# Attention, MoE and SoLU-MoE in one program: another order for the scores of the last 64 queries, two score maxima, one exponential and a weight rounding within the attention's repeating period

## The chip, the cores and the metric

The program runs on one core of a Trainium2 chip. The metric is the device time of the whole program in microseconds (us). Before the change its median is 817.85 us over 3 runs (817.72 to 817.94).

## What is computed

Three layers follow one another; only the first is touched.

```
scores = (1/sqrt(D)) * q @ k^T, causal, minus the row maximum     # B=4, H=8, S=576, D=64
a      = exp(scores); a /= a.sum(-1) + 1e-9
local  = a @ v
mem    = (phi(q) @ M_prev) / (phi(q) . z_prev + 1e-6)             # phi(x) = max(x, exp(min(x,0)) - 1) + 1
attn   = g * mem + (1 - g) * local,   g = sigmoid(beta) per head
x      = attn as (B*S, H*D)                                       # 2304 tokens x 512
x      = (h - tanh(h)) @ w_out,  h = x @ w_in                     # d_ff 2048
out    = LayerNorm(h * softmax(h)) * g_ln @ w_out2                # d_ff 1024
```

## The kernel before

**Tiling.** The 32 heads are taken in 16 pairs, two heads of 64 dimensions side by side on 128 partitions; a pair has the number i from 0 to 15. The 576 queries of a head fall into four blocks c = 0 to 3 of 128 queries and one last block of 64. The causal scores of block c are 128(c+1) wide; those of the last block are 576 wide, and both heads' 64 rows share one tile S_L. A tile of weights P carries both the index c and the head j of its pair as i = 2c + j, and i = 8 (LAST) is the tile of the last 64 queries of both heads.

**Software pipeline.** The order of all work on the attention is written out by hand, as a PROLOGUE and then a PERIOD, a list of 80 steps that `run` repeats for p = 4 to 19. A step reads `name:at:engine:part` and acts on the pair p + at. So one pass over PERIOD computes the scores of pair p-1, normalises and transposes the weights of pairs p-2 and p-3, multiplies those of p-3 with v, and stores the result of p-4. Each engine works through its own instructions in the order of that list; semaphores make it wait where a tile isn't ready.

**The steps that matter here,** in the names of the list, with the lines of the profile:

- `s_r:c` (L274, TensorE): scores of block c of both heads, each product in two passes, on halves of 64 rows of the array ("64*128" in the rows). `s_r:1` does blocks 1 and 0. `s_r:3` is 512 wide, `s_r:2` 384, `s_r:1` 256 and 128.
- `s_l` (L288, TensorE): scores of the last 64 queries, on quarters of the array ("64*64").
- `s_max:i` (L298, VectorE): adds the mask, scales, writes the scores to SBUF and takes each row's extreme. It is the reader that frees the scores' PSUM tile.
- `s_exp:i` (L320, ScalarE): the exponential with the row's maximum, and the row's sum.
- `s_eps` (L331, GpSimd) and `s_inv` (L335, VectorE): the sums plus 1e-9, and their reciprocal; part 0 is for i = 6 to 8, part 1 for i = 0 to 5.
- `s_norm:i` (L344, GpSimd): the weights times reciprocal and gate.
- `a_t:g` (L384, TensorE): transposes weights into PSUM in groups g = 0 to 5; `a_ev:g` (L391, ScalarE) copies such a group to SBUF and so frees its PSUM tile. Group 3 needs `s_norm` 3, 5 and 7, group 1 also `s_norm` 1, group 0 `s_norm` 0, 2, 4 and 6.
- `a_pv` (L408, TensorE): the transposed weights times v, into the tile X; `a_mem` (L366), `m_mm` (L225): the memory part. `x_ev` (L432): X to SBUF.
- `q_t`, `k_t` (L192, VectorE), `f_neg` (L207, GpSimd), `f_exp` (L210, ScalarE), `f_max` (L214, VectorE): q and k transposed, and phi(q) as min, exp, max.
- `w:0` to `w:8`: one conversion of a piece of MoE weights from 64-bit words into a rounded part and a remainder, in every fourth pair (i = 2, 6, 10, 14). `w:0` is on ScalarE, `w:1` to `w:5` on VectorE, `w:6` (L793) on GpSimd, `w:7` (L800, the rounding copy) on ScalarE, `w:8` (L802, the remainder) on GpSimd. `w:6` to `w:8` fall into the periods p = 6, 10, 14 and 18.
- `room`: places where the split of x for the MoE layer puts single steps (L582 on ScalarE, L584 on GpSimd).

**PSUM.** All eight banks are given out: tag S has two tiles of two banks, tag T two tiles of one bank, X one of two banks. A tile that is asked for takes the place that was given out longest ago, and the first instruction that writes it waits for the last reader of what was there. In one period, tag S is asked for by `a_t:5`, `m_mm`, `s_r:3`, `s_l`, `s_r:2`, and tag T by `a_t:0`, `a_t:2`, `a_t:4`, twice by `s_r:1` (a tile for each head), `a_t:3`, `a_t:1`. So the two tiles of `s_r:1` take the places of `a_t:2` and `a_t:4`:

```
        if c == 1:
            t = [
                self.ps.tile([P, 512], F32, tag="T", name=f"S{p}_{c}{j}", bufs=2)
                for j in range(2)
            ]
        else:
            S = self.ps.tile([P, 1024], F32, tag="S", name=f"S{p}_{c}", bufs=2)
```

After the last period the MoE layers take over; TensorE runs products for their first blocks between the last attention steps.

Of the kernel before, what the change touches and what calls it, by code (L numbers as in the profile page):

```python
# [21 lines left out]
class Attention:  # L22
# [1183 lines left out]
```

## Time and profile before

| | |
|---|---|
| median of 3 runs | 817.85 us (817.72 to 817.94) |
| the profiled execution | 813.16 us |
| its span, first to last instruction | 811.3 us |
| attention, up to its last product with v | about 210 us of the span |
| one period in the middle of it | 11.11 us |

The profile is of one execution, and its times hold for that one. "Busy" of TensorE (PE) counts matmuls whose ends are modelled; PEld are its weight loads. A row of the timeline merges neighbouring instructions of one line (x4 is four instructions), and the bracket behind it is the idle time of the engine before it, with what ended it. The chain of waits follows the work back from the last instruction, at each step to what released it. The granted clock was 0.998 of full speed.

### The profile page before, as it was taken

Reading aid. Unit: us, or ns where it says so; the run is one execution under the profiler, and the core shown is the slowest. Engines: PE = TensorE matmul, PEld = TensorE weight load, DVE = VectorE, ACT = ScalarE, POOL = GpSimd, SP = SyncE. Lnnn points to the kernel's source line nnn. Section 1 sums busy time; section 2 is a strip of 40 time slices with the busy share of each in tenths; the row PEclk is TensorE's granted clock in tenths of the full one; section 3 lists DMA queues with packets and bytes.
Section 4 is the critical chain, followed back from the end, with each engine's and each line's share of the span. In section 5 each row is a group of like instructions: output and inputs, shape, how many; then the busy total and the mean of one; then the engine's idle time right before and its main releaser. Section 6 shows DMA issues by size and latency. Waiting matters only on the chain.

```text
span 811.3 us, 13124 instructions
## 1 busy us (share of the span) xinstructions
PE 787.5 (97%) x4816; PEld 691.6 (85%) x4816; DVE 582.1 (72%) x1101; ACT 349.2 (43%) x712; POOL 375.5 (46%) x394
## 2 busy tenths in 40 slices
PE   3999999999999999999999999999999899999998
PEld 1666766666899999999999999999998688888887
DVE  5888888974377777777777777756877676767663
ACT  3788988886333333232333323232322323323322
POOL 5778898978523333233333324321542443344430
PEclk9999999999999999999999999999999999999999
DMA  8477769781012122121211212110100433333331
GB/s 176 122 171 173 155 129 162 130 168 49 23 52 78 53 57 75 53 78 53 73 58 55 76 53 78 53 53 27 53 27 27 141 106 123 111 130 112 110 116 40
DMA packets 75888, 72.57 MB, mean 89 GB/s; under 512 B 50480, under 2 KB 58416, under 8 KB 75824
## 3 DMA queue, kind: packets, MB, share of 16 engines
q1 hardware_dynamic: 75728, 71.45, 33.4%
q8 instruction: 38, 0.62, 0.3%
q10 hardware_dynamic: 96, 0.29, 0.1%
q14 instruction: 26, 0.21, 0.1%
HBM read 54.41 MB, written 12.58 MB: 83 GB/s over the span
## 4 chain that ended last, share of the span: by engine, by line
PE 87%; DVE 4%; DMA 3%; POOL 2%; ACT 2%; issue 2%; SPq 1%; DVEq 0%; ACTq 0%; POOLq 0%
PE Y L644 24%; PE H L615 24%; PE H L839 11%; PE S L274 4%; PE T L384 4%; PE X L408 4%; PE S_L L288 2%; PE R L225 2%; DVE sc L298 1%; POOL xT L584 1%; DMA v<-in_v_dram 1%; PE X L366 1%; PE O16S L939 1%; PE O1X L939 1%; PE O14X L939 1%
## 5 line engine op out<-in xcount | busy, mean ns | idle before, releaser
L644 PE MATMUL Y<-G,wo 128*128 128x384 f32 x1152 | 207.9, 335 | 0.2 <-DVE yT L656 0.2
L644 PEld LDWEIGHTS Y<-G,wo 128*128 128x128 f32 x1152 | 200.7, 188 | 0.5 <-ACT xh L582 0.4
L615 PE MATMUL H<-xh,wi 128*128 128x384 f32 x768 | 157.5, 337 | 0.0
L793 POOL TENSOR_TENSOR cvw<-cvw,cva 128x512 f32<-128x512 f32 x48 | 62.1, 1293 | 179.0 <-DVE cva L791 136.5
L615 PEld LDWEIGHTS H<-xh,wi 128*128 128x128 f32 x768 | 135.4, 188 | 1.4 <-issue 1.4
L628 ACT ACTIVATE t<-H 128x768 f32<-128x768 f32 x48 | 39.1, 814 | 211.4 <-PE H L615 211.4
L344 POOL TENSOR_SCALAR P<-P,sm,og 128x128 f32<-128x128 f32 (+3 forms) x128 | 82.0, 652 | 21.9 <-DVE sm L335 19.0
L839 PE MATMUL H<-w2i,Ys 128*128 128x512 f32 x384 | 89.9, 390 | 0.0
L615 PE MATMUL H<-xT,wi 128*128 128x384 f32 x384 | 89.7, 337 | 0.0
L839 PEld LDWEIGHTS H<-w2i,Ys 128*128 128x128 f32 x384 | 72.1, 188 | 15.0
L629 DVE TENSOR_TENSOR t<-H,t 128x768 f32<-128x768 f32 x48 | 45.9, 957 | 52.6 <-ACT t L628 52.6
L658 DVE TENSOR_TENSOR yT<-Y,yT 128x384 f32<-128x384 f32 (+1 forms) x126 | 78.9, 681 | 0.0
L631 DVE TENSOR_TENSOR G<-t,G 128x768 fp32r<-128x768 f32 x48 | 46.5, 968 | 43.3 <-ACT G L630 43.3
L320 ACT ACTIVATE P<-sc,mx 128x128 f32<-128x128 f32 (+3 forms) x128 | 70.7, 554 | 8.5 <-DVE mx L298 8.4
L298 DVE CUSTOM_DVE_ANT_0 sc<-S,mask 128x128 f32<-128x128 f32 (+3 forms) x128 | 55.5, 485 | 21.4 <-PE S L274 21.4
L615 PEld LDWEIGHTS H<-xT,wi 128*128 128x128 f32 x384 | 68.4, 188 | 0.2 <-issue 0.2
L630 ACT CAST G<-t 128x768 fp32r<-128x768 f32 x48 | 40.1, 835 | 51.2 <-DVE t L629 51.2
L391 ACT COPY pt<-T 128x512 f32<-128x512 f32 (+1 forms) x95 | 53.9, 603 | 15.9 <-PE T L384 15.5
L274 PE MATMUL S<-kT,qT 64*128 64x256 f32 (+3 forms) x256 | 46.5, 488 | 14.1 <-DVE kT L192 14.1
L871 POOL TENSOR_TENSOR s<-s,nhalf 128x1 f32<-128x1 f32 x18 | 9.9, 552 | 101.2 <-DVE s L870 92.2
L856 ACT ACTIVATE e<-H,s 128x1024 f32<-128x1024 f32 x18 | 20.1, 1116 | 80.5 <-DVE s L850 77.7
L408 PE MATMUL X<-pt,v 128*64 128x64 f32 (+4 forms) x576 | 48.2, 319 | 0.4 <-ACT pt L391 0.4
(270 smaller groups left out, 1254.6 us busy)
## 6 DMA issues: line engine op xcount, KB each, us to landing
raw<-in_moe_w_in_dram SPq DMA_DIRECT2D x24, 512.0 KB, 3.7
q<-in_q_dram SPq DMA_DIRECT2D x64, 140.0 KB, 3.0
raw<-in_moe_w_out_dram SPq DMA_DIRECT2D x16, 512.0 KB, 3.3
D<-rest SPq DMA_DIRECT2D x15, 512.0 KB, 2.6
rest<-D SPq DMA_DIRECT2D x60, 128.0 KB, 2.9
out_dram<-ob SPq DMA_DIRECT2D x17, 256.0 KB, 2.9
k<-in_k_dram SPq DMA_DIRECT2D x30, 140.0 KB, 3.6
v<-in_v_dram SPq DMA_DIRECT2D x32, 128.0 KB, 3.8
```

The source lines that it names most:

```text
L274: nc.tensor.matmul(s, Q[rows, P * r : P * r + P], K[rows, 0:w], start=True, stop=True, skip_group_check=True,)
L298: self.nc.vector.tensor_tensor_reduce(out=sc, in0=s, in1=mask, scale=-0.125, scalar=3.0e38, op0=ALU.add, op1=ALU.min, accum_out=self.mx[p] ...
L320: self.nc.scalar.activation(t, self.sc.pop((p, i)), AF.Exp, bias=self.mx[p][:, i : i + 1], scale=-1.0, accum_out=self.sm[p][:, i : i + 1],)
L344: self.nc.gpsimd.tensor_scalar(d, d, self.sm[p][:, i : i + 1], og, ALU.mult, ALU.mult)
L391: self.copy(pt, T)
L408: self.nc.tensor.matmul(self.X[j * D : (j + 1) * D, q0 : q0 + w], v[:, kb, j, :], self.pt[p, gs[j]][:, at[j] : at[j] + w], start=False, st ...
L615: nc.tensor.matmul(H[a:z, f], wi[:, wl, c, f * P + a : f * P + z], self.x[n][xl][:, c], start=(count[f] == 0), stop=(count[f] == 3 * KD - ...
L631: nc.vector.tensor_tensor(G[:, 1], t, G[:, 0].bitcast(F32), ALU.subtract)
L644: nc.tensor.matmul(Y[d][:, 0:NB], wo[:, wl, f, d * P : (d + 1) * P], G[:, gl, f], start=(i == 0), stop=(i == 3 * KF - 1),)
L658: nc.vector.tensor_tensor(y, src, y, ALU.add)
L793: self.eng.tensor_tensor(w, w, a, ALU.add)
L839: nc.tensor.matmul(H[:, nh * 512 : (nh + 1) * 512], Y[:, yl, c, :], w2i[:, wl, c, nh * 512 : (nh + 1) * 512], start=(k == 0), stop=(k == 3 ...
```

## The change

Only the text of PERIOD changes; the set of its 80 steps is the same. Five things move:

- `s_l` goes from ahead of `s_r:1` to behind `s_r:2`, and `s_r:2` goes up to stand right behind `s_r:1`. TensorE's order is `s_r:3`, `s_r:1`, `s_r:2`, `s_l` instead of `s_r:3`, `s_l`, `s_r:1`, `s_r:2`. Tag S is asked for by `s_r:2` ahead of `s_l`.
- On VectorE, `s_max:3` and `s_max:1` go ahead of `s_max:8`, and `s_inv` part 1 of the pair before goes from ahead of `s_max:8` to behind it.
- On ScalarE, `s_exp:3` goes ahead of `s_exp:8`.
- `w:7` goes from ahead of `a_ev:2` to behind `a_ev:4` on ScalarE.
- `w:8` goes from ahead of `s_eps` part 1 to behind `s_norm:3` on GpSimd.

```
-        a_ev:-3:a:1 a_t:-3:-:0 w:-4:-:6 x_ev:-4:v f_neg:-1:p a_ev:-3:a:5 s_exp:-2:-:4
-        w_ld:-2:- a_ev:-3:a:0 k_t:-1:- a_mem:-3:- s_norm:-2:-:7 w:-4:-:7 a_t:-3:-:2
-        a_ev:-3:a:2 m_eps:-2:- s_norm:-2:-:8 a_t:-3:-:4 s_r:-1:-:3 f_exp:-1:- m_inv:-2:- m_mul:-2:-
-        a_ev:-3:a:4 w:-4:-:8 s_l:-1:- s_r:-1:-:1 w:-3:-:3 room:0:-:0
-        s_eps:-2:-:1 s_norm:-2:-:6 load_q:0:s load_k:0:s s_max:-1:-:6
-        s_max:-1:-:7 m_gate:-1:- w:-2:-:0 s_exp:-1:-:6 s_exp:-1:-:7 f_max:-1:-
-        s_inv:-2:-:1 s_max:-1:-:8 s_r:-1:-:2 s_max:-1:-:3 a_pv:-3:-:0 a_pv:-3:-:3
-        a_pv:-3:-:2 s_max:-1:-:1 load_v:-2:s x_mv:-4:- s_norm:-2:-:3 w:-3:-:4
-        s_norm:-2:-:5 s_exp:-1:-:8 s_max:-1:-:2 s_max:-1:-:0 a_pv:-3:-:1 s_max:-1:-:5
-        s_norm:-2:-:1 s_max:-1:-:4 w:-2:-:1 a_t:-2:-:3 s_eps:-1:-:0 s_exp:-1:-:3
+        a_t:-3:-:0 w:-4:-:6 x_ev:-4:v f_neg:-1:p a_ev:-3:a:5 s_exp:-2:-:4 w_ld:-2:-
+        a_ev:-3:a:0 k_t:-1:- a_mem:-3:- s_norm:-2:-:7 a_t:-3:-:2 a_ev:-3:a:2 m_eps:-2:-
+        s_norm:-2:-:8 a_t:-3:-:4 s_r:-1:-:3 f_exp:-1:- m_inv:-2:- m_mul:-2:- a_ev:-3:a:4
+        w:-4:-:7 s_r:-1:-:1 s_r:-1:-:2 w:-3:-:3 room:0:-:0 s_eps:-2:-:1 s_norm:-2:-:6
+        load_q:0:s load_k:0:s s_max:-1:-:6 s_max:-1:-:7 s_l:-1:- m_gate:-1:- w:-2:-:0
+        s_exp:-1:-:6 s_exp:-1:-:7 f_max:-1:- s_max:-1:-:3 s_max:-1:-:1 s_exp:-1:-:3
+        s_max:-1:-:8 s_inv:-2:-:1 a_pv:-3:-:0 a_pv:-3:-:3 a_pv:-3:-:2 load_v:-2:s x_mv:-4:-
+        s_norm:-2:-:3 w:-4:-:8 w:-3:-:4 s_norm:-2:-:5 s_exp:-1:-:8 s_max:-1:-:2 s_max:-1:-:0
+        a_pv:-3:-:1 s_max:-1:-:5 s_norm:-2:-:1 s_max:-1:-:4 w:-2:-:1 a_t:-2:-:3 s_eps:-1:-:0
```

## Rows read from the trace of the kernel before

**Rows 1.** The page, part 1: busy time, share of span, instructions.

```profile
PE 787.5 (97%) x4816; PEld 691.6 (85%) x4816; DVE 582.1 (72%) x1101; ACT 349.2 (43%) x712; POOL 375.5 (46%) x394
```

**Rows 2.** Chain of waits, period p = 4: start us, us, what.

```profile
43.93 1.12 PE S_L L288 x8
...
55.04 1.12 PE S_L L288 x8
```

**Rows 3.** Timeline of TensorE, p = 5: start, us, instructions, idle before.

```profile
49.37 1.09 PE L384 MATMUL T<-ident,P 128*128 128x128 f32 x8
...
53.91 1.13 PE L274 MATMUL S<-kT,qT 64*128 64x512 f32 x4
54.97 1.19 PE L288 MATMUL S_L<-kT,qT 64*64 64x512 f32 x8
56.09 1.57 PE L274 MATMUL S<-kT,qT 64*128 64x256 f32 x12
57.59 2.96 PE L408 MATMUL X<-pt,v 128*64 128x512 f32 x36
```

**Rows 4.** Timeline of ScalarE, p = 5: `a_ev:2`, `f_exp`, `a_ev:4`.

```profile
53.58 0.59 ACT L391 COPY pt<-T 128x512 f32<-128x512 f32 x1 [0.34 <-PE T L384]
54.06 0.69 ACT L210 ACTIVATE e<-e 128x576 f32<-128x576 f32 x1
54.65 0.58 ACT L391 COPY pt<-T 128x512 f32<-128x512 f32 x1
```

**Rows 5.** Chain of waits, p = 11: TensorE resumes behind a copy.

```profile
120.08 0.48 ACT pt L391
...
120.61 0.66 PE T L384 x4
```

**Rows 6.** Timeline of VectorE, p = 5: `s_max:7`, `s_inv:1`, `s_max:8`.

```profile
55.70 0.69 DVE L298 CUSTOM_DVE_ANT_0 sc<-S,mask 128x512 f32<-128x512 f32 x1
...
56.99 0.18 DVE L335 RECIPROCAL sm<-sm 128x6 f32<-128x6 f32 x1
57.09 0.71 DVE L298 CUSTOM_DVE_ANT_0 sc<-S_L,maskL 128x576 f32<-128x576 f32 x1
```

**Rows 7.** Timeline of GpSimd, p = 5 and 6: `s_norm` 3, 5, 1; `f_neg`; `w:8`.

```profile
57.27 1.80 POOL L344 TENSOR_SCALAR P<-P,sm,og 128x256 f32<-128x256 f32 x3 [0.82 <-DVE sm L335]
...
62.84 1.65 POOL L207 TENSOR_SCALAR e<-qT 128x576 f32<-128x576 f32 x1
...
66.01 1.28 POOL L802 TENSOR_TENSOR wi<-cvw,wi 128x512 fp32r<-128x512 f32 x1
```

**Rows 8.** Timeline of GpSimd, p = 9 and 10: the same `s_norm` and `f_neg`.

```profile
102.11 1.80 POOL L344 TENSOR_SCALAR P<-P,sm,og 128x256 f32<-128x256 f32 x3 [0.82 <-DVE sm L335]
...
108.65 1.64 POOL L207 TENSOR_SCALAR e<-qT 128x576 f32<-128x576 f32 x1
```

**Rows 9.** Timeline of ScalarE: `a_ev:4` of p = 9, `f_exp` of p = 10.

```profile
99.09 0.58 ACT L391 COPY pt<-T 128x512 f32<-128x512 f32 x1
...
110.32 0.68 ACT L210 ACTIVATE e<-e 128x576 f32<-128x576 f32 x1 [0.52 <-POOL e L207]
```

**Rows 10.** Who waited for whom: us in total, times, longest us.

```profile
ACT e L210 <- POOL e L207: 9.1, 3, 8.0
```

**Rows 11.** Timeline of TensorE, end of p = 10 to p = 11.

```profile
116.03 1.09 PE L384 MATMUL T<-ident,P 128*128 128x128 f32 x8
...
120.61 0.66 PE L384 MATMUL T<-ident,P 128*128 128x128 f32 x4 [0.40 <-ACT pt L391]
121.19 1.13 PE L274 MATMUL S<-kT,qT 64*128 64x512 f32 x4
```

**Rows 12.** Timeline of ScalarE, p = 18: `w:7`, then `a_ev:2` and `a_ev:4`.

```profile
206.56 0.62 ACT L800 CAST wo<-cvw 128x512 fp32r<-128x512 f32 x1 [1.04 <-POOL cvw L793]
207.09 1.07 ACT L391 COPY pt<-T 128x512 f32<-128x512 f32 x2
```

**Rows 13.** Timeline of TensorE, p = 18: the products behind those copies.

```profile
208.21 1.52 PE L408 MATMUL X<-pt,v 128*64 128x256 f32 x12 [0.35 <-ACT pt L391]
```

More of the change, by code (lines that the diff above doesn't have):

```diff
@@ L473 @@
         q_t:-1:- s_norm:-3:-:4 w:-3:-:2 s_exp:-2:-:0 s_exp:-2:-:5 s_norm:-3:-:0 a_t:-3:-:5
-        s_norm:-3:-:2 m_mm:-2:- room:0:-:2 a_ev:-3:a:3 load_m:-1:- s_inv:-2:-:0
-        a_ev:-3:a:1 a_t:-3:-:0 w:-4:-:6 x_ev:-4:v f_neg:-1:p a_ev:-3:a:5 s_exp:-2:-:4
-        w_ld:-2:- a_ev:-3:a:0 k_t:-1:- a_mem:-3:- s_norm:-2:-:7 w:-4:-:7 a_t:-3:-:2
-        a_ev:-3:a:2 m_eps:-2:- s_norm:-2:-:8 a_t:-3:-:4 s_r:-1:-:3 f_exp:-1:- m_inv:-2:- m_mul:-2:-
-        a_ev:-3:a:4 w:-4:-:8 s_l:-1:- s_r:-1:-:1 w:-3:-:3 room:0:-:0
-        s_eps:-2:-:1 s_norm:-2:-:6 load_q:0:s load_k:0:s s_max:-1:-:6
-        s_max:-1:-:7 m_gate:-1:- w:-2:-:0 s_exp:-1:-:6 s_exp:-1:-:7 f_max:-1:-
-        s_inv:-2:-:1 s_max:-1:-:8 s_r:-1:-:2 s_max:-1:-:3 a_pv:-3:-:0 a_pv:-3:-:3
-        a_pv:-3:-:2 s_max:-1:-:1 load_v:-2:s x_mv:-4:- s_norm:-2:-:3 w:-3:-:4
-        s_norm:-2:-:5 s_exp:-1:-:8 s_max:-1:-:2 s_max:-1:-:0 a_pv:-3:-:1 s_max:-1:-:5
-        s_norm:-2:-:1 s_max:-1:-:4 w:-2:-:1 a_t:-2:-:3 s_eps:-1:-:0 s_exp:-1:-:3
+        s_norm:-3:-:2 m_mm:-2:- room:0:-:2 a_ev:-3:a:3 load_m:-1:- s_inv:-2:-:0 a_ev:-3:a:1
+        a_t:-3:-:0 w:-4:-:6 x_ev:-4:v f_neg:-1:p a_ev:-3:a:5 s_exp:-2:-:4 w_ld:-2:-
[7 more added lines that the diff above has]
+        a_pv:-3:-:1 s_max:-1:-:5 s_norm:-2:-:1 s_max:-1:-:4 w:-2:-:1 a_t:-2:-:3 s_eps:-1:-:0
         a_t:-2:-:1 s_exp:-1:-:2 w:-3:-:5 s_exp:-1:-:1
```

## The prediction

> **What bounds the kernel now.** First the page's busy times [rows 1]: TensorE is busy for 97% of the span, no other engine for more than 72%. That is an average over three layers, so the next view is the chain of waits inside the attention. It runs through TensorE alone for whole periods, and the same step comes back after 55.04 - 43.93 = 11.11 us [rows 2]. TensorE's timeline then shows its instructions of one period end to end without a bracket of idle time [rows 3]. In such a period nothing that another engine saves is worth anything; the period grows by whatever TensorE waits, and shrinks only by what TensorE no longer does. The third view is therefore the waits that stand close behind TensorE: the copies of ScalarE that free PSUM [rows 4], the maxima on VectorE [rows 6] and the GpSimd queue [rows 7, 8]. There are 13 periods, p = 4 to 16, in which scores are computed by PERIOD's order.
>
> **Part 1: the order of the scores on TensorE.** Three things come of it.
>
> *A wait is added.* The two tiles of `s_r:1` take the places of `a_t:2` and `a_t:4`, so its product for the second head can't start before `a_ev:4` has read its place. Before, `s_l` stood between; now `s_r:1` follows `s_r:3` directly, and that ends where `s_l` starts today, at 54.97 [rows 3]. `a_ev:4` ends at 54.65 + 0.58 = 55.23 [rows 4]. It can't be earlier: `a_ev:2` starts when its transposes end (its bracket names them), `f_exp` and `a_ev:4` follow end to end. A resumption of TensorE behind such a copy took 120.61 - (120.08 + 0.48) = 0.05 us [rows 5]. So `s_r:1` restarts at 55.28. Then come `s_r:1` and `s_r:2` with 57.59 - 56.09 = 1.50 and `s_l` with 56.09 - 54.97 = 1.12 [rows 3], and `a_pv` starts at 57.90 instead of 57.59: **+0.31 per period, 13 x 0.31 = +4.0**. Behind the waiting instruction stand `s_r:2`, which is ready, `s_l` and `a_pv`; all of TensorE waits with it.
>
> *A switch falls away, if the wait doesn't eat it.* `s_r:3` streams 2 x 512 columns in 53.91 to 54.97 = 1.06 us, `s_r:1` and `s_r:2` together 2 x (256 + 128 + 384) = 1536 in 1.50 [rows 3]. So 512 columns cost 0.44, and each group has 0.18 that isn't streaming: the turn from another division of the array and the first weight load. With `s_r:1` right behind `s_r:3`, both on halves, that 0.18 could go. But a load that waits for `a_ev:4` isn't hidden, so I keep the full 1.50. The bounds: 0.31 if nothing is hidden, 0.31 - 0.18 = 0.13 if all is. I take 0.31, since the wait sits on the first pair of products. The Trainium skill says under "TensorEngine Tiling (Array Packing)", Key Properties, that changing the tiling mode, not just the tile, drains TensorE. The row's 0.18 agrees with that; by this rule alone one drain fewer would be worth 13 x 0.18 = 2.3 us, and it speaks for the change.
>
> *Later readers.* `s_l` now takes the place of `s_r:3` in tag S and waits for `s_max:7`, which ends at 55.70 + 0.69 = 56.39 [rows 6]; `s_l` comes at 55.28 + 1.50 = 56.78, so this is hidden. `a_t:5` now waits for `s_max:4` in place of `s_max:8`. `s_max:8` ends some 3.45 us behind the restart (below), `a_t:5` comes at 5.5 + 1.0 (8 transposes, 1.09 with their tail [rows 3]); 3.0 us hold `s_inv` and four maxima, none as wide as the 0.71 of `s_max:8`. Hidden too.
>
> **Part 2: the maxima and the reciprocal.** `s_max:8` now waits for `s_l`, which ends at 56.78 + 1.19 = 57.97 instead of 54.97 + 1.19 = 56.16. `s_max:3`, `s_max:1` and `s_exp:3` fill the gap on VectorE and ScalarE and cost nothing. What stands behind `s_max:8` is `s_inv:1`, and GpSimd waits for it ahead of `s_norm` 3, 5 and 1: the bracket of 0.82 [rows 7]. The new time: 57.97 + 0.05 + 0.71 for `s_max:8`, then 57.27 - 56.99 = 0.28 from `s_inv` to `s_norm:3` [rows 6, 7], is 59.0 instead of 57.27. So GpSimd's queue starts **1.7 later in the period**, 3.7 behind the restart. In a normal period this is hidden by GpSimd's idle time. In periods with `w:6` it isn't, since `w:6` stands ahead of `f_neg`, `f_exp` waits for `f_neg`, and `a_ev:4` stands behind `f_exp`:
>
> - p = 6: `f_neg` ends at 62.84 + 1.65 + 1.7 = 66.19 [rows 7]; `f_exp` would start at 54.06 + 11.11 + 0.31 = 65.48 [rows 4]. **+0.7**.
> - p = 10: `a_ev:4` of p = 9 ends at 99.67, so the restart is at 99.72 and `s_norm:3` at 103.42 instead of 102.11: 1.3 later. `f_neg` ends at 108.65 + 1.64 + 1.3 = 111.59 [rows 8, 9]; `f_exp` would start at 99.09 - 0.59 + 11.11 + 0.31 = 109.92. **+1.7**. Already today `f_exp` waits 0.52 there [rows 9], at no cost, because `s_l` covers it.
> - p = 14: the wait for `f_neg` occurs three times, 8.0 of 9.1 us in one of them [rows 10], so the other two are alike. **+1.7**.
>
> **Part 3: the rounding behind the copies.** `w:7` behind `a_ev:4` takes 0.62 us of ScalarE [rows 12] from ahead of `a_ev:2`; in p = 11 and 15 TensorE now loses 121.19 - 116.03 = 5.16 against 53.91 - 49.37 = 4.54, so 0.62 [rows 11, 3], because the maxima and copies run late behind a conversion. I count it all as given back: **-1.2**. In p = 18 the products wait 0.35 for copies that stand behind `w:7` [rows 12, 13]: **-0.35**.
>
> `w:8` now stands between `s_norm:3` and `s_norm:5`, and `a_t:3` at the end of the period needs `s_norm:5`. Counted from the restart: 3.7 + 0.6 (a third of 1.80) + 1.28 + 0.6 = 6.2 [rows 7]; `a_t:3` wants to start at 1.50 + 1.12 + 2.89 = 5.5 (49.37 + 11.11 - 57.59 is the 2.89) [rows 3]. **+0.7 in each of p = 6, 10 and 14: +2.1**. Whether `f_neg` of the next period is then late as well, these rows leave open: 0 to 0.7 each.
>
> No DMA step changes its place on SP's queue, and none is moved past.
>
> **The sum.** 4.0 + (0.7 + 1.7 + 1.7) + 2.1 - 1.2 - 0.35 = +8.65, so +8.6 us. The profiled execution takes 813.16 us with a span of 811.3, so it would become 821.8 with a span of 819.9. The median of the runs is 4.7 above the profiled one; with the same distance it is 817.85 + 8.6 = **826.4**.
>
> **The rivals.**
>
> - *The wait alone.* If GpSimd's queue catches up (its `s_norm` of 1.80 hold stretches in which they share with VectorE, and these would fall elsewhere), parts 2 and 3 add nothing: 4.0 - 1.2 - 0.35 = +2.4, **820.2**. For it: normal periods have idle time on GpSimd [rows 7]; against it: p = 10 is late already today [rows 9].
> - *No wait: the maxima become the bound.* If `a_ev:4` is in time, `s_r:1` and `s_r:2` end at 54.97 + 1.50 - 0.18 = 56.29, `s_l` waits for `s_max:7` until 56.44 and ends at 57.56: -0.03 per period, -0.4. With the stalls given back, -0.4 - 1.2 - 0.35 = -2.0, **815.9**. It decides at an end of `a_ev:4` ahead of 54.97, and it is 0.26 later in the row; only a `f_exp` that goes elsewhere would change that. By the drain rule above with all of its 2.3, the time would be 817.85 - 3.9 = 814.0.
> - *The hidden load.* With 0.13 in place of 0.31 and no late GpSimd: 1.7 - 1.2 - 0.35 = +0.1, **818.0**.
>
> The wait rests on program order: a TensorE instruction that waits isn't passed. In p = 11 TensorE stands idle for 0.40 ahead of `a_t:4` [rows 11], and nothing behind it goes ahead. The Trainium skill states it so under "TensorE: Matmul & The Clock Gate", Part 2, step-by-step: matmuls stay in program order, and only weight loads are pulled ahead. Were it otherwise, `s_r:2` would fill the wait and the +0.31 would shrink towards nothing.
>
> **How the numbers follow.** The forecast has 0.58, the wait alone 0.25, no wait 0.10, the hidden load 0.07. A measurement of this kernel can tell 0.2%, 1.6 us, from no change. So slower has 0.83, same 0.07, faster 0.10. The range reaches down to the wait alone, 820.0, and up by the open lateness of `f_neg`, 3 x 0.7 = 2.1, with a little for the rest: 829.0.
>
> **What would show it.** In the timeline of the changed kernel, the first rows of L274 behind the 512-wide ones should carry a bracket that names ACT pt L391, of 0.2 to 0.4 in most periods; the period in the chain should be 11.4 instead of 11.11; in p = 6, 10 and 14 `f_exp` should wait for `f_neg`, and `a_t:3` for GpSimd's weights. The prediction is wrong if the period stays at 11.11 or below, if `a_ev:4` no longer ends behind `s_r:3`, or if those three periods cost no more than the others.

## The result and the profile after

| | before | after |
|---|---|---|
| median | 816.23 us (6 runs, 813.60 to 817.94) | **824.58 us** (6 runs, 822.86 to 825.67) |
| ratio after to before | | **1.0111**, 95% interval 1.0086 to 1.0137 |
| profiled execution | 813.16 us | 822.87 us |
| its span | 811.3 us | 821.0 us |
| second group of Y products starts (attention done) | 214.93 us | 224.65 us |
| from there to the end | 596.4 us | 596.4 us |

(Three of before's six runs are those of the table ahead of the prediction; the ratio is taken from runs that stand beside each other, and stands for 9.1 us where the two medians differ by 8.35.) The changed kernel is slower by about 1%, and all of it lies in the attention. The page of after, part 1, busy time by engine, shows next to nothing of it:

```profile
PE 793.7 (97%) x4816; PEld 697.3 (85%) x4816; DVE 579.5 (71%) x1101; ACT 351.3 (43%) x712; POOL 376.3 (46%) x394
```

The share of 97% is that of [rows 1], and PE's busy time even grew, by 6.2 us: the page doesn't tell a loss of this kind. The chain of waits of after, in p = 4 and 5 (start us, us, what), says more:

```profile
44.03 2.86 PE S L274 x14
46.89 1.12 PE S_L L288 x8
...
55.44 2.86 PE S L274 x14
```

The step that came back after 11.11 us in [rows 2] comes back after 55.44 - 44.03 = 11.41. All scores of the row blocks take 2.86 where `s_r:3` and the group of `s_r:1` and `s_r:2` took 1.06 + 1.50 = 2.56 [rows 2, 3]: 0.30 more.

TensorE's timeline of after (start, us, instructions, idle before) at the scores of p = 6 and of p = 10, and behind those:

```profile
66.78 1.55 PE L274 MATMUL S<-kT,qT 64*128 64x512 f32 x6
68.67 1.56 PE L274 MATMUL S<-kT,qT 64*128 64x256 f32 x10 [0.33 <-ACT pt L391]
...
113.78 1.55 PE L274 MATMUL S<-kT,qT 64*128 64x512 f32 x6
116.63 1.56 PE L274 MATMUL S<-kT,qT 64*128 64x256 f32 x10 [1.30 <-ACT pt L391]
118.12 1.19 PE L288 MATMUL S_L<-kT,qT 64*64 64x512 f32 x8
119.24 2.96 PE L408 MATMUL X<-pt,v 128*64 128x512 f32 x36
122.13 0.33 PE L384 MATMUL T<-ident,P 128*128 128x128 f32 x1
122.83 1.08 PE L384 MATMUL T<-ident,P 128*128 128x128 f32 x7 [0.38 <-POOL P L344]
```

Four products of `s_r:3` and the two of `s_r:1`'s first head run (x6); the second head's wait for the copy `a_ev:4`, and the ten that are left still take 118.12 - 116.63 = 1.49. In p = 10 there is a second wait, of `a_t:3` for GpSimd's weights. ScalarE's timeline of after shows `a_ev:2`, `f_exp` and `a_ev:4` of those two periods:

```profile
66.45 0.58 ACT L391 COPY pt<-T 128x512 f32<-128x512 f32 x1 [0.34 <-PE T L384]
67.46 0.68 ACT L210 ACTIVATE e<-e 128x576 f32<-128x576 f32 x1 [0.42 <-POOL e L207]
68.05 0.57 ACT L391 COPY pt<-T 128x512 f32<-128x512 f32 x1
...
113.44 0.58 ACT L391 COPY pt<-T 128x512 f32<-128x512 f32 x1 [0.34 <-PE T L384]
115.42 0.68 ACT L210 ACTIVATE e<-e 128x576 f32<-128x576 f32 x1 [1.39 <-POOL e L207]
116.01 0.57 ACT L391 COPY pt<-T 128x512 f32<-128x512 f32 x1
```

`f_exp` waits 0.42 and 1.39 for `f_neg` and holds up `a_ev:4`, which ends at 68.62 and 116.58; TensorE goes on 0.05 later each time, as in [rows 5]. On GpSimd, `s_norm:3` of p = 5 starts late, behind the moved `s_inv:1`, and `f_neg` of p = 6 and 10 ends at 67.43 and 115.38:

```profile
60.44 1.69 POOL L344 TENSOR_SCALAR P<-P,sm,og 128x256 f32<-128x256 f32 x3 [1.01 <-DVE sm L335]
...
65.77 1.66 POOL L207 TENSOR_SCALAR e<-qT 128x576 f32<-128x576 f32 x1
...
113.74 1.64 POOL L207 TENSOR_SCALAR e<-qT 128x576 f32<-128x576 f32 x1
```

Who waited for whom in after, against [rows 10] (us in total, times, longest us):

```profile
ACT e L210 <- POOL e L207: 11.7, 6, 8.0
...
PEld S L274 <- ACT pt L391: 10.3, 26, 1.7
```

The second row is new: two weight loads in each of 13 periods.

**A finer measure than the median.** Within one execution a period without a special wait repeats to 0.01 or 0.02 us, while runs of one kernel spread over some 5 us. So the distance between the starts of successive 512-wide scores (the L274 rows that begin with 64x512, as at 66.78 and 113.78 above) is what the experiments are read by. In us, from one period to the next:

| kernel | normal | 6 to 7 | 9 to 10 | 10 to 11 | 11 to 12 | 14 to 15 |
|---|---|---|---|---|---|---|
| before | 11.11 | 11.11 | 11.11 | 11.73 | 11.11 | 11.74 |
| after | 11.41 | 12.62 | 11.55 | 13.59 | 11.75 | 13.58 |
| e1 | 11.41 | 11.49 | 11.41 | 12.41 | 11.41 | 12.41 |
| e2 | 11.41 | 11.41 | 11.41 | 12.39 | 11.41 | 12.44 |
| e3 | 11.41 | 11.94 | 11.55 | 12.90 | 11.41 | 12.90 |
| e4 | 11.11 | 11.35 | 11.11 | 11.99 | 11.11 | 12.00 |
| e5 | 11.11 | 11.11 | 11.11 | 11.15 | 11.11 | 11.14 |
| e6 | 11.09 | 11.78 | 11.12 | 12.22 | 11.09 | 12.22 |
| e7 | 11.09 | 11.09 | 11.09 | 11.40 | 11.09 | 11.39 |
| e8 | 11.09 | 12.01 | 11.09 | 12.96 | 11.12 | 12.96 |
| e9 | 11.37 | 11.45 | 11.51 | 12.41 | 11.38 | 12.40 |
| e10 | 11.11 | 11.11 | 11.11 | 11.17 | 11.11 | 11.16 |
| e11 | 10.91 | 11.11 | 11.40 | 11.10 | 10.91 | 12.06 |

Conversions fall into p = 6, 10 and 14. Of the distances that the table leaves out, 13 to 14 is like 9 to 10 and 15 to 16 like 11 to 12, and one other stands out by over 0.1: 5 to 6, with 11.27 in e7, 11.54 in e9 and 11.27 in e11.

### The profile page after: what moved, and what is told of

It is laid out like the page before. It is cut to its first block, busy times and chain, and to the rows that moved or that the text cites. A ratio compares the mean times of both kernels' runs of the same rounds, so it can differ in the third digit from the quotient of the medians.

```text
span 821.0 us, 13114 instructions
## 1 busy us (share of the span) xinstructions
PE 793.7 (97%) x4816; PEld 697.3 (85%) x4816; DVE 579.5 (71%) x1101; ACT 351.3 (43%) x712; POOL 376.3 (46%) x394
## 4 chain that ended last, share of the span: by engine, by line
PE 85%; POOL 7%; DVE 3%; issue 3%; ACT 1%; DMA 1%; SPq 0%; DVEq 0%; POOLq 0%; ACTq 0%
PE Y L643 24%; PE H L614 24%; PE H L838 11%; PE S L274 4%; PE T L384 4%; PE X L408 3%; POOL P L344 3%; PE S_L L288 2%; PE R L225 1%; POOL xT L583 1%; POOL e L207 1%; PE X L366 1%; PE O16S L938 1%; PE O1X L938 1%; PE O14X L938 1%
## 5 line engine op out<-in xcount | busy, mean ns | idle before, releaser
L274 PE MATMUL S<-kT,qT 64*128 64x128 f32 (+3 forms) x256 | 51.3, 493 | 17.6 <-DVE kT L192 14.4
L274 PEld LDWEIGHTS S<-kT,qT 64*128 64x128 f32 x256 | 27.0, 204 | 33.3 <-DVE kT L192 13.2
```

Source lines behind the costliest of these rows:

```text
L274: nc.tensor.matmul(s, Q[rows, P * r : P * r + P], K[rows, 0:w], start=True, stop=True, skip_group_check=True,)
```

## The experiments

All of them compute the whole reference; only the order of steps in PERIOD differs (in e11 in PROLOGUE too).

**e1, the order alone.** Before's PERIOD with the new order of scores, maxima and exponential; `s_inv:1`, `w:7` and `w:8` keep their places of before.

```diff
-a_ev:-3:a:4 w:-4:-:8 s_l:-1:- s_r:-1:-:1
+a_ev:-3:a:4 w:-4:-:8 s_r:-1:-:1 s_r:-1:-:2
...
+s_max:-1:-:7 s_l:-1:-
...
-f_max:-1:- s_inv:-2:-:1 s_max:-1:-:8 s_r:-1:-:2 s_max:-1:-:3
+f_max:-1:- s_inv:-2:-:1 s_max:-1:-:3 s_max:-1:-:1 s_exp:-1:-:3 s_max:-1:-:8
...
```

> From the kernel before, only the scores' order and the maxima and the exponential that follow it are changed (s_r:3, s_r:1, s_r:2, s_l; s_max:3, s_max:1, s_exp:3 ahead of s_max:8); s_inv:1, w:7 and w:8 stay where they were before. Theory: the wait of s_r:1 for a_ev:4 alone costs 13 x 0.30 = 3.9 us, and in p = 6, 10 and 14, where a_ev:4 is later behind w:7, another 0.1 + 0.7 + 0.7; so +3.9 to +5.4 against before, and the period is 11.41 in the trace. Rival (GpSimd's late queue is what costs, the order itself is free or a gain): 0 to -2.4, period 11.11 or below.

Measured: 1.0064 (1.0041 to 1.0086), 819.22 against 813.65 us. The normal period has the full +0.30, so the order isn't free. In p = 10 and 14 another 1.00 comes without any step of part 2 or 3. TensorE's timeline of e1 at p = 10, and `a_t:2` and `a_t:4` of p = 11:

```profile
112.56 1.55 PE L274 MATMUL S<-kT,qT 64*128 64x512 f32 x6
114.93 1.56 PE L274 MATMUL S<-kT,qT 64*128 64x256 f32 x10 [0.81 <-ACT pt L391]
116.42 1.19 PE L288 MATMUL S_L<-kT,qT 64*64 64x512 f32 x8
...
124.00 1.04 PE L384 MATMUL T<-ident,P 128*128 128x128 f32 x8
```

In before `f_exp` waits 0.52 there too [rows 9], but `s_l` stood between `s_r:3` and the place that `a_ev:4` frees. Taking it away makes an old, covered lateness visible: two thirds of the 1.48 that p = 10 of after loses by late copies on top of the 0.30 of every period. The scores up to `s_l` take 116.42 - 112.56 = 3.86 here instead of 2.86, which is all of the 1.00. So the stall of before ahead of `a_t:4` in p = 11, 0.62 long with a bracket of 0.40 [rows 11], is gone in e1: the row at 124.00 holds the eight transposes of `a_t:2` and `a_t:4` without a bracket. `w:7` and `w:8` stand there as in before, so the new order of scores is enough to remove the stall.

**e2, the reciprocal back up.** After, with `s_inv:1` right behind `f_max`.

```diff
-f_max:-1:- s_max:-1:-:3 s_max:-1:-:1 s_exp:-1:-:3 s_max:-1:-:8 s_inv:-2:-:1
+f_max:-1:- s_inv:-2:-:1 s_max:-1:-:3 s_max:-1:-:1 s_exp:-1:-:3 s_max:-1:-:8
```

> The changed kernel with s_inv:1 back ahead of the maxima (right behind f_max). Theory: GpSimd's queue starts 1.7 us earlier, f_exp waits for f_neg no longer in p = 6 and by only 0.4 in p = 10 and 14, and w:8 is done in time for s_norm:5, so a_t:3 waits no longer; left are 13 x 0.30 + 0.8 - 1.2 - 0.35 = +3.1 against before. Rival (the conversion's remainder w:8 itself is what is too long for the queue, wherever the reciprocal stands): f_exp and a_t:3 go on waiting, +6 to +8.5.

Measured: p = 6 falls from 12.62 to 11.41, p = 10 from 13.59 to 12.39, p = 14 from 13.58 to 12.44. The span is 815.4, 4.1 above before. By the runs it is 1.0081 (1.0056 to 1.0105), with 820.08, 820.98 and 820.19 us beside the profiled 817.23; the section on the clock has the likely reason why single executions differ by that much. So the place of `s_inv:1` makes GpSimd late, and this costs 1.2 us in each conversion. The 1.0 that is left in p = 10 and 14 was expected at 0.4; it is the uncovered lateness of e1. From e1, e2 differs only in the places of `w:7` and `w:8`, and their distances from p = 6, 10 and 14 agree within 0.08: in the new order these two moves are worth next to nothing as long as `s_inv:1` is early. TensorE of e2 in p = 11 shows that `a_t:3` no longer waits, although `w:8` has after's place:

```profile
116.14 2.96 PE L408 MATMUL X<-pt,v 128*64 128x512 f32 x36
119.03 1.09 PE L384 MATMUL T<-ident,P 128*128 128x128 f32 x8
```

**e3, the remainder right behind the rounding.** After, with `w:8` behind `w:7` instead of behind `s_norm:3`.

```diff
-a_ev:-3:a:4 w:-4:-:7 s_r:-1:-:1
+a_ev:-3:a:4 w:-4:-:7 w:-4:-:8 s_r:-1:-:1
...
-s_norm:-2:-:3 w:-4:-:8 w:-3:-:4
+s_norm:-2:-:3 w:-3:-:4
```

> The changed kernel with w:8 taken from between s_norm:3 and s_norm:5 and put right behind w:7, where GpSimd's queue waits for s_inv:1 anyway. Theory: a_t:3 no longer waits in p = 6, 10 and 14 (0.69 each in the changed kernel's trace) and f_neg of p = 11 and 15 is no longer late (0.34 each): 2.7 less than the changed kernel, the periods of p = 6, 10, 14 at 11.9, 12.9, 12.9 instead of 12.62, 13.59, 13.58; the other periods stay at 11.41. Rival (the wait of a_t:3 comes from the late s_inv:1 alone): 0.0, the same periods.

Measured: 1.0087 (1.0055 to 1.0119); 11.94, 12.90 and 12.90. So 12.62 - 11.94 = 0.68 and twice 0.69 are `w:8`'s place, and so are the 0.34 of p = 11 and 15. Against e2 the rest of `s_inv:1`'s cost is 11.94 - 11.41 = 0.53 and 12.90 - 12.39 = 0.51. The wait of `a_t:3` takes both moves: it is gone in e2, where the queue is early, and in e3, where `w:8` is out of it.

**e4, the rounding alone,** and **e5, the remainder alone,** each from before.

```diff
 e4
-s_norm:-2:-:7 w:-4:-:7 a_t:-3:-:2
+s_norm:-2:-:7 a_t:-3:-:2
...
-a_ev:-3:a:4 w:-4:-:8 s_l:-1:-
+a_ev:-3:a:4 w:-4:-:7 w:-4:-:8 s_l:-1:-
 e5
-a_ev:-3:a:4 w:-4:-:8 s_l:-1:-
+a_ev:-3:a:4 s_l:-1:-
...
-s_norm:-2:-:3 w:-3:-:4
+s_norm:-2:-:3 w:-4:-:8 w:-3:-:4
```

> The kernel before with w:7 alone moved behind a_ev:4; w:8 stays behind it at its place. Theory of the prediction (the 0.62 us that TensorE loses in p = 11 and 15 is of w:7's making): -1.2 - 0.35 = -1.6 against before, and the bracket ahead of a_t:4 there is gone. Rival (it is of w:8's making, which stands ahead of s_eps:1 on GpSimd and makes s_inv:1 and with it all maxima late): -0.35 only, the bracket stays.

> The kernel before with w:8 alone moved behind s_norm:3. Theory of the prediction (the loss of 0.62 us in p = 11 and 15 is of w:7's making): 0.0 against before, the bracket ahead of a_t:4 stays. Rival (w:8 ahead of s_eps:1 makes it): -1.2, the bracket is gone. Both: s_norm:5 is late for a_t:3 by nothing here, since s_inv:1 stands ahead of s_max:8.

Measured: e4 1.0023 (1.0007 to 1.0039), e5 0.9994 (0.9976 to 1.0012). Moving `w:7` alone makes p = 6, 10 and 14 **longer** by 0.24 to 0.26, a loss that neither its theory nor the rival foresaw; it comes to 0.76, and what else the 1.9 us of its ratio hold isn't shown. Moving `w:8` alone takes 0.58 and 0.60 of the 0.62 out of p = 10 and 14. So in the order of before the stall that the prediction laid to `w:7` came from `w:8`. VectorE's timeline of before in p = 10, `f_max`, `s_inv:1` and `s_max:8`:

```profile
111.87 1.83 DVE L214 SCALAR_TENSOR_TENSOR f<-qT,e 128x576 f32<-128x576 f32 x1
113.85 0.19 DVE L335 RECIPROCAL sm<-sm 128x6 f32<-128x6 f32 x1
113.96 0.72 DVE L298 CUSTOM_DVE_ANT_0 sc<-S_L,maskL 128x576 f32<-128x576 f32 x1
```

GpSimd's timeline of before beside it, `w:8` and `s_eps:1`:

```profile
111.82 1.27 POOL L802 TENSOR_TENSOR wi<-cvw,wi 128x512 fp32r<-128x512 f32 x1
113.16 0.66 POOL L331 TENSOR_SCALAR sm<-sm 128x6 f32<-128x6 f32 x1
```

The same three on VectorE in e5:

```profile
111.81 0.75 DVE L214 SCALAR_TENSOR_TENSOR f<-qT,e 128x576 f32<-128x576 f32 x1
112.70 0.19 DVE L335 RECIPROCAL sm<-sm 128x6 f32<-128x6 f32 x1
112.81 0.72 DVE L298 CUSTOM_DVE_ANT_0 sc<-S_L,maskL 128x576 f32<-128x576 f32 x1
```

In before, `f_max` starts 0.05 behind `w:8`, takes 1.83 and ends at 113.70, 0.61 behind `w:8`'s end. `s_eps:1`, which stands behind `w:8` on GpSimd, ends at 113.82, and `s_inv:1`, which needs it, starts 0.03 later, so of the two it is `s_eps:1` that comes last. `s_max:8` follows late: it starts 113.96 - 109.46 = 4.50 behind `s_r:3` in before and 112.81 - 109.40 = 3.41 behind it in e5. The Trainium skill says under "SBUF — State Buffer", Who interferes with whom, that a VectorE instruction with two SBUF inputs contends with a GpSimd instruction that reads SBUF, that the pair of ports they share is an exclusive lock, and that issue order decides who blocks. These rows agree: 1.83 for the `f_max` that started behind `w:8`, 0.75 in e5 where `w:8` isn't. In e4, with `w:7` ahead of it, `w:8` starts later, and this time `f_max` is first (at 110.79, with 0.75) and `w:8` takes 1.66 instead of 1.27. Then `s_eps:1` waits for `w:8`, and `s_inv:1` for `s_eps:1`; on GpSimd and VectorE of e4:

```profile
111.02 1.66 POOL L801 TENSOR_TENSOR wi<-cvw,wi 128x512 fp32r<-128x512 f32 x1 [0.30 <-ACT wi L799]
...
113.04 0.19 DVE L335 RECIPROCAL sm<-sm 128x6 f32<-128x6 f32 x1 [1.49 <-POOL sm L331]
113.14 0.72 DVE L298 CUSTOM_DVE_ANT_0 sc<-S_L,maskL 128x576 f32<-128x576 f32 x1
```

With `s_r:3` of e4 at 108.39 that is 4.75, 0.25 later than in before, which is what p = 10 grew by (11.99 - 11.73 = 0.26). The stall is there with a short `f_max` too, so `w:8`'s place ahead of `s_eps:1` is enough for it; what the long `f_max` adds in before isn't shown apart.

**e10, both conversion moves without the scores' order,** from before.

```diff
-s_norm:-2:-:7 w:-4:-:7 a_t:-3:-:2
+s_norm:-2:-:7 a_t:-3:-:2
...
-a_ev:-3:a:4 w:-4:-:8 s_l:-1:-
+a_ev:-3:a:4 w:-4:-:7 s_l:-1:-
...
-s_norm:-2:-:3 w:-3:-:4
+s_norm:-2:-:3 w:-4:-:8 w:-3:-:4
```

> The kernel before with both steps of the conversion moved and nothing else: w:7 behind a_ev:4, w:8 behind s_norm:3. Theory: w:8's move gives back 0.6 each in p = 10 and 14, and with w:8 off the path w:7 behind the copies costs nothing more (alone it cost 0.25 in three periods, because w:8 and s_eps:1 came later by it); the last products no longer wait 0.35. Periods 11.11, against before -1.2 - 0.35 = -1.6. Rival (w:7 costs behind the copies by itself, in ScalarE's order): p = 6, 10 and 14 at 11.35, -0.8 or less.

Measured: 0.9994 (0.9977 to 1.0010). In the trace p = 10 and 14 are 11.17 and 11.16, and the way from p = 16's `s_r:3` to the second Y group falls from 37.55 to 36.97, by 0.58. So in the tail, too, the copies of p = 18 gain more than the bracket of 0.35 [rows 13]. Together 0.56 + 0.58 + 0.58 = 1.7 us of gain, no more than the runs can tell from nothing.

**e6, `f_exp` behind `a_ev:4`,** from after. This takes away what makes the copy late.

```diff
-s_r:-1:-:3 f_exp:-1:- m_inv:-2:- m_mul:-2:- a_ev:-3:a:4 w:-4:-:7
+s_r:-1:-:3 m_inv:-2:- m_mul:-2:- a_ev:-3:a:4 f_exp:-1:- w:-4:-:7
```

> The changed kernel with f_exp moved from ahead of a_ev:4 to behind it, so that the copy ends 0.6 us earlier and ahead of the end of s_r:3. Theory: s_r:1 no longer waits, the period falls from 11.41 to 11.08, where s_l waits for s_max:7; f_neg's lateness in p = 6, 10, 14 no longer reaches TensorE, w:8 still costs 0.69 in each; against before -0.4 + 2.1 - 1.2 - 0.35 = +0.1. Rival by the drain rule (a turn of the array fewer, worth its full 0.18): period 10.93, -1.8 against before. Rival (the wait is not the copy's): period stays at 11.41.

Measured: 1.0015 (0.9996 to 1.0033), and a normal period of 11.09. The +0.30 is gone, and no more than 0.02 is gained below before. TensorE's timeline of e6, p = 5, and the wait of `a_t:3` that stays in p = 11:

```profile
54.01 2.43 PE L274 MATMUL S<-kT,qT 64*128 64x512 f32 x16
56.55 1.19 PE L288 MATMUL S_L<-kT,qT 64*64 64x512 f32 x8
57.67 2.96 PE L408 MATMUL X<-pt,v 128*64 128x512 f32 x36
...
117.88 1.08 PE L384 MATMUL T<-ident,P 128*128 128x128 f32 x7 [0.80 <-POOL P L344]
```

Who waited for whom in e6:

```profile
PEld S_L L288 <- DVE mx L298: 10.5, 14, 1.0
```

The 16 products of the row blocks take 2.43 less a tail of 0.07 (in [rows 3] a row of 1.13 stands for 1.06), so 2.36 instead of 1.06 + 1.50: 0.20 less. But `s_l` starts 56.55 - 54.01 - 2.36 = 0.18 late, since it now waits for `s_max:7`. This is the prediction's second rival, which it put at 11.08. The wait of `a_t:3` costs the expected 0.69 in p = 6, but 1.13 in p = 10 and 14, where its bracket is 0.80; why it is longer there isn't shown.

**e8, block 2 between,** from after: `s_r:2` ahead of `s_r:1`.

```diff
-s_r:-1:-:3 f_exp:-1:- m_inv:-2:- m_mul:-2:- a_ev:-3:a:4 w:-4:-:7 s_r:-1:-:1 s_r:-1:-:2
+s_r:-1:-:3 s_r:-1:-:2 f_exp:-1:- m_inv:-2:- m_mul:-2:- a_ev:-3:a:4 w:-4:-:7 s_r:-1:-:1
```

> The changed kernel with s_r:2 ahead of s_r:1 (s_r:3, s_r:2, s_r:1, s_l), nothing else. Theory: the 0.64 us of s_r:2 cover the 0.35 by which a_ev:4 is late; the period falls from 11.41 to 11.08 to 11.11, and only the lateness beyond it is left in p = 6 (0.3), 10 and 14 (1.2 each), beside the 0.69 of w:8 in each; against before about -0.4 + 2.7 + 2.1 - 1.2 - 0.35 = +2.8. Rival (what costs in the new order is not the place of the second head's tile but the row of scores without s_l between): period 11.41 as in the changed kernel.

Measured: 1.0038 (1.0016 to 1.0060); 11.09 in normal periods. The lateness of `f_neg` still shows in p = 10, in TensorE's timeline of e8:

```profile
110.27 2.20 PE L274 MATMUL S<-kT,qT 64*128 64x512 f32 x10
113.13 0.92 PE L274 MATMUL S<-kT,qT 64*128 64x256 f32 x6 [0.66 <-ACT pt L391]
```

A product that is ready put into the wait fills it, as a program order without overtaking would have it.

**e7, all of it mended,** from after: `f_exp` behind `a_ev:4`, `s_inv:1` right behind `f_max`, `w:8` behind `s_norm:1`.

```diff
-s_r:-1:-:3 f_exp:-1:- m_inv:-2:- m_mul:-2:- a_ev:-3:a:4 w:-4:-:7
+s_r:-1:-:3 m_inv:-2:- m_mul:-2:- a_ev:-3:a:4 f_exp:-1:- w:-4:-:7
...
-f_max:-1:- s_max:-1:-:3 s_max:-1:-:1 s_exp:-1:-:3 s_max:-1:-:8 s_inv:-2:-:1
+f_max:-1:- s_inv:-2:-:1 s_max:-1:-:3 s_max:-1:-:1 s_exp:-1:-:3 s_max:-1:-:8
...
-s_norm:-2:-:3 w:-4:-:8 w:-3:-:4
+s_norm:-2:-:3 w:-3:-:4
...
-s_norm:-2:-:1 s_max:-1:-:4
+s_norm:-2:-:1 w:-4:-:8 s_max:-1:-:4
```

> The changed kernel's order of scores with three steps mended: f_exp behind a_ev:4, s_inv:1 ahead of s_max:3, w:8 behind s_norm:1. Theory: no wait of TensorE is left but that of s_l for s_max:7; all periods at 11.08, p = 10 and 14 as well; against before -0.4 - 1.2 - 0.35 = -2.0. Rival (drain rule in full): all periods at 10.93, -3.9. Rival (GpSimd's queue is too long in p = 10 and 14 in any order): those two at 11.7 or more, -0.8 or worse.

Measured: 0.9998 (0.9982 to 1.0014). All of the loss is given back and nothing more: with the copies early, the maxima are the bound of the normal period, 11.09. In p = 10 and 14, where 11.08 was expected as well, it is 11.40 and 11.39: in p = 11 the four products of `a_t:0` take 0.91 instead of 0.60, and three of their weight loads wait 0.32 for GpSimd's weights.

**e9, block 2 ahead,** from e7: `s_r:2`, `s_r:3`, `s_r:1`, `s_l`, and the maxima in the order in which the scores come. Then `s_l` needs no late maximum.

```diff
-s_r:-1:-:3 m_inv:-2:- m_mul:-2:- a_ev:-3:a:4 f_exp:-1:- w:-4:-:7 s_r:-1:-:1 s_r:-1:-:2
+s_r:-1:-:2 s_r:-1:-:3 m_inv:-2:- m_mul:-2:- a_ev:-3:a:4 f_exp:-1:- w:-4:-:7 s_r:-1:-:1
...
-s_max:-1:-:6 s_max:-1:-:7 s_l:-1:-
+s_max:-1:-:5 s_max:-1:-:4 s_inv:-2:-:1 s_max:-1:-:6 s_max:-1:-:7 s_l:-1:-
...
```

> The kernel with three steps mended, and the scores in the order s_r:2, s_r:3, s_r:1, s_l, with s_max:5 and s_max:4 first and s_inv:1 between them and s_max:6. Now s_l takes the place of s_r:2, whose two readers of 0.55 us are done while s_r:3 and s_r:1 run, so s_l should wait for nobody. Theory by the drain rule (one turn of the array fewer is worth its full 0.18): all periods at 10.93, against before 13 x -0.18 - 1.2 - 0.35 = -3.9. Rival (the turn's 0.18 is not saved, since s_l still has to turn to quarters and back): periods at 11.05 to 11.11, -1.6 to -2.4.

Measured: 1.0049 (1.0029 to 1.0070), and a normal period of 11.37. TensorE's timeline of e9, p = 5:

```profile
53.72 0.66 PE L384 MATMUL T<-ident,P 128*128 128x128 f32 x4 [0.19 <-ACT pt L391]
54.30 2.43 PE L274 MATMUL S<-kT,qT 64*128 64x384 f32 x16
56.66 1.19 PE L288 MATMUL S_L<-kT,qT 64*64 64x512 f32 x8
57.78 2.96 PE L408 MATMUL X<-pt,v 128*64 128x512 f32 x36
```

All scores take 57.78 - 54.30 = 3.48, against 57.59 - 53.91 = 3.68 in [rows 3]. So a turn of the array between halves and quarters is worth 0.20 where nobody waits. The Trainium skill's rule under "TensorEngine Tiling (Array Packing)", Key Properties, that a change of tiling mode drains TensorE, agrees with this. But `a_t:4` now waits for a copy in every period, and the period is longer all the same. The reading, which e11 tests, is that the late maxima of block 3 make ScalarE's exponentials and copies late.

**e11, two exponentials earlier as well,** from e9: `s_exp:5` and `s_exp:4` of pair p - 1 run ahead of `s_exp:6`.

```diff
-s_exp:-2:-:0 s_exp:-2:-:5 s_norm:-3:-:0
+s_exp:-2:-:0 s_norm:-3:-:0
...
-a_ev:-3:a:5 s_exp:-2:-:4 w_ld:-2:-
+a_ev:-3:a:5 w_ld:-2:-
...
-w:-2:-:0 s_exp:-1:-:6 s_exp:-1:-:7
+w:-2:-:0 s_exp:-1:-:5 s_exp:-1:-:4 s_exp:-1:-:6 s_exp:-1:-:7
...
 PROLOGUE
-s_max:2:-:4 s_eps:2:-:0
+s_max:2:-:4 s_exp:2:-:5 s_exp:2:-:4 s_eps:2:-:0
```

> The kernel with s_r:2, s_r:3, s_r:1, s_l in that order, and s_exp:5 and s_exp:4 run in the period of their maxima, ahead of s_exp:6, instead of at the start of the next one. In the trace of the order alone, the scores up to a_pv take 3.48 us instead of 3.68, so a turn fewer does give its 0.2, but a_t:4 then waits 0.2 to 0.4 for a copy, because ScalarE's exponentials come late. Theory: with two exponentials moved into ScalarE's idle time the copies are in time, the period is 10.91, and against before 13 x -0.2 - 1.2 - 0.35 = -4.1. Rival (ScalarE or VectorE is the bound in any order): a wait stays ahead of a_t:4 or a_t:5, periods above 11.1, no gain.

Measured: 1.0015 (1.0004 to 1.0026), a little slower than before. TensorE's timeline of e11, p = 7 and 8, and the last period:

```profile
77.30 2.43 PE L274 MATMUL S<-kT,qT 64*128 64x384 f32 x16
...
88.21 2.43 PE L274 MATMUL S<-kT,qT 64*128 64x384 f32 x16
...
189.07 1.38 PE L225 MATMUL R<-MZ,f 128*128 128x130 f32 x10 [1.93 <-ACT pt L391]
```

A period of 88.21 - 77.30 = 10.91 shows that the 0.20 can be had. But p = 5, 9, 13 and 14 have waits (11.28, 11.40, 11.33 and 12.06), and at the end of the attention `m_mm` waits 1.93 for a copy. None of the versions beats the kernel before by more than the runs can tell.

## Why the prediction held, step by step

The forecast was +8.6 and 826.4 us; the medians moved by 824.58 - 816.23 = 8.35 us, to 824.58. The time itself came out 1.8 below 826.4 mainly because the forecast was counted from 817.85, the median of three runs, and six runs put before at 816.23. Term by term, from the distances above:

| step of the prediction | said | measured |
|---|---|---|
| `s_r:1` waits for `a_ev:4`, 13 periods | 13 x 0.31 = 4.0 | 13 x 0.30 = 3.9 |
| late `f_neg` in p = 6, 10, 14 | 0.7, 1.7, 1.7 | 0.52, 1.48, 1.47 |
| `a_t:3` waits for `s_norm:5` | 3 x 0.7 | 3 x 0.69 |
| late `f_neg` in the next period, left open | 3 x (0 to 0.7) | 0.34 in p = 11 and in p = 15 |
| nothing foreseen | | 0.14 in p = 9 and in p = 13 |
| stalls of p = 10 and 14 given back | -1.2 | -1.25 |
| tail, p = 18 | -0.35 | -0.6 |
| sum | 8.65 | 8.55 |

(The tail from p = 16's `s_r:3` to the second Y group went from 37.55 to 37.25 with the 0.30 of p = 16 in it, so by -0.6 without it. The 0.14: in p = 9 and 13 a step of the split of x stands ahead of `f_neg`, and `f_exp` comes 0.14 later behind `s_r:3` than in p = 5.) The profiled span grew by 9.7. The other 1.16 lies in the PROLOGUE, whose text is the same (see "The clock" below).

The chain of causes held, but that the sum came within 0.1 is in part luck. The three terms of the late `f_neg` and the gain of the tail were off by 0.9 together in one direction, and 0.96 that was left open or not foreseen came in the other.

- **The wait, right.** `s_r:1` waits for `a_ev:4`, with the releaser, the price and the restart of 0.05 that were named; e1 shows it without the other parts, and e6 takes it away by its cause. That the whole 1.50 had to be kept was right as well: the ten products that are left take 1.49. The two of the first head that slip in ahead of the wait gain nothing. They hide part of it, though: the brackets of 0.2 to 0.4 that were to show in most periods don't. In normal periods the 16 products stand in one row, and only the chain and the waits of the weight loads tell of the wait.
- **The rivals.** The wait alone (820.2) fell, because GpSimd didn't catch up: `s_norm:3` started 60.44 - 56.78 = 3.66 behind the restart (55.37 for `s_r:3`, 1.06 for it, 0.35 to the copy's end), and 3.7 was predicted. The hidden load (818.0) fell by the 1.49. The maxima as the bound weren't reached in after, but that rival's own condition, an `f_exp` that goes elsewhere, was tried in e6 and gave 11.09 for its 11.08.
- **The late queue, right in its chain, too large by 0.2 each.** The prediction shifted the whole queue by 1.7 in p = 6. In after, `s_norm:3` to the end of `f_neg` takes 67.43 - 60.44 = 6.99 instead of 64.49 - 57.27 = 7.22 [rows 7]; other work of VectorE runs beside it there, but that this is the reason isn't shown. In p = 10, too, part of the shift was lost on the way, 115.38 - 107.44 = 7.94 instead of 110.29 - 102.11 = 8.18 [rows 8]. There the prediction's 1.7 held 0.4 of lateness that is there without any shift (`f_neg` ends at 110.29, `f_exp` would start at 109.92) and 1.3 of the shift. The runs divide it the other way: e1 has 1.00 of the 1.48 without the shift, which leaves 0.48 for the reciprocal's place. So here two wrong sizes nearly made up for each other.
- **The stall given back, right in size and wrong in cause.** The step "`w:7` behind `a_ev:4` takes 0.62 us of ScalarE [rows 12] from ahead of `a_ev:2`; in p = 11 and 15 TensorE now loses ... 0.62" fails: that the 0.62 of the cast and the 0.62 of the stall are equal was chance. e4 moves `w:7` and loses 0.25; e5 moves `w:8` and has the 0.6. The rows that would have told it were in the trace of before, `f_max` at 1.83 beside `w:8` and `s_eps:1` right behind `w:8`, and the prediction didn't use them. And in the changed kernel neither move was needed for it: e1, with both steps at their old places, has no stall any more. Why the new order alone removes it isn't shown; TensorE comes 1.00 later to those copies there. So the 1.25 is a difference between before and after that the order of the scores brings by itself.
- **The tail, right in cause and too small.** The 0.35 was laid to `w:7`, and that holds: with `w:8` alone moved (e5) the bracket is still 0.34 and the way from p = 16's `s_r:3` to the second Y group 37.52, with both moved (e10) there is no bracket and it is 36.97. The bracket of 0.35 [rows 13] was taken as the price. The whole stretch of `a_pv` shrank from 209.66 - 206.19 = 3.47 in before to 219.37 - 216.48 = 2.89 in after, 0.58. It is the same at the end of p = 10 in before, where a bracket of 0.40 [rows 11] cost 0.62.

## What to carry to other kernels

Where one engine runs end to end, read from its timeline what stands between two instructions that share a buffer, before you reorder them: `s_l`'s 1.12 us covered a copy 0.26 to 0.35 late in every period and a queue 0.5 late in two, and taking it away cost more than the turn of the array that it saved. Price a wait by the distance between two recurring starts and not by its bracket. And when a stall has the length of an instruction nearby, move that instruction alone before you name it as the cause, and see whether another part of the change takes the stall away by itself.

## What the runs showed of the hardware that was not expected

**The clock.** Stretches at half clock lie in other places from one execution to the next. The views by windows (stretch, us, busy time of PE, PEld, DVE, ACT and POOL, PEclk, DMA share, GB/s) of the start of before:

```profile
19.00:24.00 5.00, 4.97 (x24) 2.60 (x24) 3.39 (x14) 2.00 (x6) 3.53 (x6) 0.67 0.78 186
24.00:29.00 5.00, 3.52 (x34) 3.01 (x30) 4.96 (x14) 4.56 (x15) 4.18 (x6) 1.00 0.00 2
```

of after:

```profile
19.00:24.00 5.00, 5.00 (x18) 2.75 (x20) 2.80 (x12) 2.09 (x5) 3.53 (x6) 0.50 0.78 178
24.00:29.00 5.00, 4.69 (x35) 3.31 (x31) 4.29 (x15) 3.41 (x10) 2.90 (x5) 0.91 0.00 2
```

and, far behind the attention, of e4:

```profile
630.00:635.00 5.00, 2.48 (x11) 1.70 (x10) 4.20 (x8) 0.97 (x2) 0.55 (x1) 0.98 0.37 105
635.00:640.00 5.00, 4.39 (x10) 3.47 (x11) 3.54 (x7) 2.28 (x5) 3.60 (x2) 0.50 0.46 158
```

0.50 is the lower level, 1.2 GHz, 1.00 the upper, 2.4 GHz. In after the low stretch at the start lasts longer, and the scores of p = 4 begin at 43.96 instead of 42.80. Of the kernels with that PROLOGUE they begin at 41.48 in e4, at 42.70 to 42.94 in before, e2, e3, e5, e6, e8 and e9, and at 43.77 to 44.08 in after, e1, e7 and e10, with no regard to what was changed. So the 1.16 is taken as the execution's, not the change's; one trace of each can't prove it. Behind the attention, the same work takes 596.4 to 596.5 us in eight of the traces and 596.7 in e3, but 598.0 in e5 and e11 and 599.4 to 599.5 in e7 and e4. In e4 TensorE was busy for 2.48 of the 5 us ahead of the fall to 0.50. What sets these stretches stays open. Their effect of 1 to 3 us is of the size of most differences studied here, so only the distances between periods could settle them.

**A bracket is less than the price of its wait.** In after, brackets of 0.33 and 1.30 at `s_r:1` stand in periods that lose 0.30 + 0.52 = 0.82 and 0.30 + 1.48 = 1.78 there: 0.49 and 0.48 more. At `a_t:4` and `a_pv` of before it is 0.62 for 0.40 and 0.58 for 0.35. In p = 6 of after, the six products that run before the wait take 1.55 and the ten behind it 1.49: 3.04 without the bracket, where the 16 took 2.56 in before. A likely reason is that work which overlapped (the two products that could start, the load of the first weights) no longer does and that no bracket counts it; no run tests this.
